# Full segments alone: half 0's memory sums in four matmuls, the sums' banks exchanged, token sums by halves, a quarter of the second values on VectorE

## The chip, the cores and the metric

The kernel runs on one core of one Trainium2 chip. The metric is the device time of one execution in microseconds (us). TensorE is called PE in the profile's lines (PEld are its weight loads), VectorE is DVE, ScalarE ACT, GpSimd POOL and SyncE SP.

## The reference

Two layers, each an attention with a recurrent memory and then a gated mixer over the sequence; inputs are bf16, the sequence has 2048 tokens of width 512.

```python
def _A_ref(x, mem0, Wq, Wk, Wv, Wo, seg_len):        # 32 heads of 128, 8 memory rows, seg_len 32
    mem = mem0
    for s in range(n_seg):                            # 64 segments, one after the other
        h = jnp.concatenate([mem, x[:, s*seg_len:(s+1)*seg_len]], axis=1)      # 40 rows
        q, k, v = (jnp.einsum('btd,dhe->bhte', h, W) for W in (Wq, Wk, Wv))
        scores = jnp.einsum('bhqe,bhke->bhqk', q, k) * Dh ** (-0.5)
        p = _softmax(jnp.where(mask[None, None], scores, -1e9), axis=-1)
        o = jnp.einsum('bhte,hed->btd', jnp.einsum('bhqk,bhke->bhqe', p, v), Wo)
        mem = o[:, :M, :]                             # the memory of the next segment
        outs.append(o[:, M:, :])
...
x = x + _A_ref(_layernorm(x), ...)
x = x + _B_ref(_layernorm(x), ...)                    # gated mixer over the sequence
x = x + _A_ref(_layernorm(x), ...)
x = x + _B_ref(_layernorm(x), ...)
```

The mask lets each row see the 8 memory rows and the tokens up to itself. The softmax needs, for every head and query row, the sum of the exponentials over the keys; that sum is what the change touches.

## The kernel before, in words

The attention pass `a_block` runs twice (`first` is true for the first pass). It goes through 64 segments (`s`), four to a block of 128 rows (`tb = s // 4`, `j4 = s % 4`, 16 blocks). A segment needs the memory rows that the segment before it left, so segments run one after the other. TensorE, VectorE and ScalarE run their instructions in the order in which the program issues them. The order within a segment is written out by hand in `segment`, with work of the next block or of the output product put between its steps: three calls of `fill()` take such work from a generator. In full segments (below) they yield 4, 8 and 20 matmuls of 512 columns.

The 32 heads are handled as two halves `r` of 16 heads. In a segment, in order:

- queries and keys of both halves (`qk`, into `psQ`, `psm`, `psK`), copied by ScalarE and turned by VectorE;
- scores of half 0 into `psS`, ScalarE's exponential into `S` (`exps`, L1123), VectorE's mask product into `E` (`close`, L1126); values of half 0 from `psK` to `VA[:, 0]` by VectorE (L1212);
- values of half 1 into `psV` in four steps over the contraction, with the scores of half 1 and then `sums_zero` (L1137) between them. `sums_zero` sums half 0's exponentials for the 8 memory query rows: sixteen matmuls on 128x32 tiles with the constant `half`, into the free end of the `psS` bank;
- ScalarE: logarithm of those sums (`inverse`, L1180), copy of half 1's values to `VA[:, 1]` (L1227), exponential of minus the logarithm (L1181), which gives their inverse in `Rm`; VectorE: `close(1)`;
- the first `fill()`; `pv(0)`, the product of weights and values of half 0 (L1163, and L1166 for the memory rows' keys), into `psO[0]`; `sums_tokens` (L1155), the sums of both halves for the token rows into `psT`, four matmuls on 64x128 tiles with the constant `ones`; `sums_one` (L1146), the memory sums of half 1, four such matmuls, into the columns 320 to 384 of `psO[1]`; `pv(1)` into `psO[1]`;
- VectorE's `memory_out(0)` (L1184), the memory rows of half 0 times `Rm`, into `uT`; `spare1`, work of other blocks on VectorE and GpSimd; the second `fill()`; ScalarE's `inverse` of half 1; `memory_out(1)`;
- the output product of the memory rows: `wo_pairs` (L946, half 0's heads, into `px`) and `wo_rest` (L953, half 1's heads, into columns 384 to 512 of `psO[1]`); then the fold of its parts, the next segment's memory rows, and the token rows (`tok_out`, `last_out`).

Each of `psO[0]` and `psO[1]` is a pair of PSUM banks. The framework puts a wait between instructions of different engines that touch the same PSUM memory; where the kernel knows better it says so by hand. Line 1055 does that for two copies out of `px` that read different partitions, one by ScalarE and one by VectorE:

```python
m = nc.vector.tensor_copy(cross[64:128, :], px[0:64, 128:256])
tc.declare_no_dep(m.ins, beside.ins, reason="other partitions of the tile")
```

In the first pass some blocks take parts of their product from an earlier stage:

```python
light = first and tb + 1 < NB and (tb + 1) // 4 in EARLY        # EARLY = (2, 3)
```

Of the kernel before, what the change touches and what calls it, by code (L numbers as in the profile page):

```python
# [717 lines left out]
def a_block(tc, c, rows, front, MV_in, RS_in, MV_out, RS_out, ahead, wo, S, first):  # L718
    nc = tc.nc
# [5 lines left out]
    with ExitStack() as ctx:  # L725
# [39 lines left out]
        def other_bank(mms, *reads):  # L765

            for m in mms:
                for r in reads:
                    tc.declare_no_dep(m.ins, r.ins, reason="another bank of the tile")
# [301 lines left out]
        def segment(s, fill, spare1, spare2, spare3, tail, loads):  # L1071
# [21 lines left out]
            def v_mm(r, ps, kts=range(KT)):  # L1093
                return mm_chunk(ps, lambda kt, cg: hA_cur[:, kt, :], lambda kt, cg: cols_rhs(w, 4 + r, kt, cg), kts)
# [30 lines left out]
            def close(r):  # L1125
                nc.vector.tensor_tensor(out=E[:, r], in0=S[:, r].unsqueeze(1).to_broadcast([P, 2, 224]), in1=maskN[:], op=ALU.mult)  # L1126

            def e_all(e, lo, hi):

                return e[:, :, 0:160].rearrange("p n (i q) -> p n i q", q=40)[:, :, :, lo:hi]  # L1130

            def e_own(e, b):
                return e[:, :, 160:224].rearrange("p n (i b e) -> p n i b e", i=4, b=2)[:, :, :, b, :]

            def sums_zero(pN):

                return [nc.tensor.matmul(pN[32 * cg:32 * cg + 32, 64 * g:64 * g + 64], lhsT=half[:, g, :], rhs=e_own(E[:, 0], 0) if k else e_all(E[:, 0], 0, 8),  # L1137
                                         start=False, stop=True, tile_position=(0, 32 * cg), skip_group_check=True)
                        for k in range(2) for g in range(2) for cg in range(4)]

            def sums_one():

                for k in range(2):
                    for g in range(2):
                        e = E[64 * g:64 * g + 64, 1]
                        nc.tensor.matmul(psO[1][:, g, 320:384], lhsT=ones[64 * g:64 * g + 64, :], rhs=e_own(e, 0) if k else e_all(e, 0, 8),  # L1146
                                         start=(k == 0), stop=True, skip_group_check=True)

            def sums_tokens(ps):

                for k in range(2):
                    for g in range(2):
                        e = E[64 * g:64 * g + 64].rearrange("p r s n -> p (r s) n")
                        o = ps[:, g, :].rearrange("p (n i q) -> p n i q", n=4, i=4)
                        nc.tensor.matmul(o[:, :, :, 24:32] if k else o, lhsT=ones[64 * g:64 * g + 64, :],  # L1155
                                         rhs=e_own(e, 1) if k else e_all(e, 8, 40), start=(k == 0), stop=True, skip_group_check=True)

            def pv(r):

                for i in range(4):  # L1160
                    for g in range(2):
                        o = psO[r][:, g, 0:320].rearrange("p (s i q) -> p s i q", s=2, i=4)[:, :, i, :]
                        nc.tensor.matmul(o, lhsT=VA[64 * g:64 * g + 64, r, i, :], rhs=E[64 * g:64 * g + 64, r, :, 40 * i:40 * i + 40],  # L1163
                                         start=(r == 0 and i == 0), stop=True, skip_group_check=True)
                for g in range(2):
                    nc.tensor.matmul(ends(heads40(psO[r][:, g, 0:320])), lhsT=VX[64 * g:64 * g + 64, j4, r, :],  # L1166
                                     rhs=E[64 * g:64 * g + 64, r, :, 160:224], start=False, stop=True, skip_group_check=True)
# [10 lines left out]
            def inverse(r, src):  # L1178
                rm = Rm[:, r]
                nc.scalar.activation(out=rm, in_=src, func=ACT.Ln)  # L1180
                return lambda: nc.scalar.activation(out=rm, in_=rm, func=ACT.Exp, scale=-1.0)  # L1181
# [26 lines left out]
            expd = exps(0)  # L1208
# [10 lines left out]
            other_bank(scores(1), expd)  # L1219
            expd = exps(1)  # L1220
            v_mm(1, psW, (2,))
            pN = psS[:, 0, 224:352]
            other_bank(sums_zero(pN), expd)
            v_mm(1, psW, (3,))
            Rm = segp.tile([P, 2, 2, 64], F32, name="Rm", bufs=1)
            invert = inverse(0, pN.rearrange("p (g q) -> p g q", g=2))
            nc.scalar.copy(VA[:, 1].rearrange("p i e -> p (i e)"), psW[:])  # L1227
# [101 lines left out]
        for s in range(NSEG):  # L1329
# [164 lines left out]
```

## Time and profile before

| | |
|---|---|
| median of 3 runs | 1601.4 us (1600.6 to 1609.43) |
| the profiled execution's own time | 1603.44 us |
| its span, first to last instruction | 1601.7 us |
| mean granted TensorE clock | 0.998 |

In the page, the first block gives each engine's busy time and its share of the span. The chain of waits is followed back from the last instruction: at each step to what released it, or to the instruction before it on its engine. In lists in order of time each line has the start and the length in us, the engine, the kernel's line, the operation, the tiles (out<-in), shapes and the count of instructions put together; a bracket gives idle time of the engine before it and what ended it. TensorE's matmuls are pipelined, so their lengths overlap.

### The profile page before, as it was taken

To read this page: it belongs to the slowest core of one execution; us is meant where nothing else is said; L and a number is where in the kernel's file an instruction comes from. 1 tells how busy PE (TensorE), PEld (TensorE's weight loads), DVE (VectorE), ACT (ScalarE), POOL (GpSimd) and SP (SyncE) were. 2 spreads that over 40 slices of the span, in tenths; PEclk is the share of its full clock that TensorE was granted. 3 is DMA by queue.
4 is the path that set the end of the run, shared out by engine and by line. 5 is a ranking of instruction groups with operands and counts; after the bars stand their busy time and mean duration, and the time that the engine had idled before them with its cause. 6 is when DMAs were issued, how large, how long until landed. Compare 5 with 4: busy or idle time off the path is not lost.

```text
span 1601.7 us, 90904 instructions
## 1 busy us (share of the span) xinstructions
PE 1578.5 (99%) x41046; PEld 977.2 (61%) x41046; DVE 1086.1 (68%) x3094; ACT 1050.9 (66%) x2279; POOL 306.8 (19%) x674
## 2 busy tenths in 40 slices
PE   7999999999999999999999999999999999999999
PEld 3566666666666666666656666666666666665565
DVE  4666777777777777784456666666777677767722
ACT  4677777777777777670057777777777777776400
POOL 6211121112211222320021111111222122224000
PEclk9999999999999999999999999999999999999999
DMA  9322111122211332378951111111222123416697
GB/s 361 132 58 42 44 40 37 44 41 80 74 53 41 87 87 61 102 177 170 207 170 45 45 48 48 41 40 41 67 86 67 40 66 87 89 50 179 146 193 163
DMA packets 240540, 145.99 MB, mean 91 GB/s; under 512 B 173272, under 2 KB 215872, under 8 KB 240152
## 3 DMA queue, kind: packets, MB, share of 16 engines
q1 hardware_dynamic: 226232, 94.00, 25.9%
q0 software_dynamic: 13920, 46.18, 8.6%
q8 instruction: 321, 5.26, 1.3%
q14 instruction: 67, 0.55, 0.1%
HBM read 60.21 MB, written 39.55 MB: 62 GB/s over the span
## 4 chain that ended last, share of the span: by engine, by line
PE 94%; DMA 2%; DVE 2%; issue 1%; ACT 1%; POOL 0%; DVEq 0%; SPq 0%; POOLq 0%; ACTq 0%
PE psQ L762 14%; PE psK L762 13%; PE psb L762 10%; PE pg L403 9%; PE psO L953 7%; PE px L946 7%; PE psm L762 7%; PE psV L762 7%; PE pwB L965 3%; PE psO L1163 3%; PE pz L302 3%; PE psT L1155 2%; PE py L446 2%; PE psS L1114 2%; PE psS L1137 1%; PE psO L1166 1%
## 5 line engine op out<-in xcount | busy, mean ns | idle before, releaser
L762 PEld LDWEIGHTS <-hT 128*32 128x32 bf16 x12288 | 339.4, 97 | 262.3 <-DVE hT L1063 18.3
L762 PE MATMUL psV<-Wv_sb,hT 128*32 128x512 bf16 x2048 | 165.8, 379 | 0.0
L1088 ACT CAST rows<-psQ 128x512 bf16<-128x512 f32 x256 | 144.3, 589 | 21.2 <-PE psQ L762 17.5
L1184 DVE TENSOR_TENSOR uT<-psO,Rm 128x128 bf16<-128x128 f32 x256 | 74.7, 292 | 122.7 <-ACT Rm L1181 121.6
L1123 ACT ACTIVATE S<-psS 128x224 bf16<-128x224 f32 x256 | 92.2, 360 | 97.4 <-PE psS L1118 97.4
L1091 DVE STREAM_TRANSPOSE KA<-rows 128x256 f32<-128x256 f32 x256 | 113.0, 441 | 61.9 <-ACT rows L1088 59.4
L403 PE MATMUL pg<-z,wspT 128*128 128x344 bf16 x1024 | 154.3, 310 | 0.0
L1187 DVE TENSOR_TENSOR uT<-psO,Rt 128x384 bf16<-128x384 f32 x256 | 140.3, 548 | 18.8 <-ACT Rt L1266 17.4
L762 PE MATMUL psK<-Wv_sb,hT 128*32 128x512 bf16 x2048 | 151.7, 378 | 0.0
L1266 ACT ACTIVATE Rt<-Rt 128x512 f32<-128x512 f32 x256 | 147.3, 622 | 4.0
L1091 DVE STREAM_TRANSPOSE QQ<-rows 128x256 f32<-128x256 f32 x256 | 112.5, 440 | 49.0 <-ACT rows L1088 46.1
L953 PE MATMUL psO<-Wo_high,uT 128*32 128x128 bf16 x8192 | 140.5, 220 | 2.1 <-issue 1.1
L762 PE MATMUL psQ<-Wq_sb,hT 128*32 128x512 bf16 x2048 | 135.0, 380 | 0.5 <-issue 0.5
L946 PE MATMUL px<-Wo,uT 128*32 128x256 bf16 x3840 | 134.7, 274 | 0.3
L762 PE MATMUL psQ<-Wk_sb,hT 128*32 128x512 bf16 x2048 | 134.6, 379 | 0.0
L762 PE MATMUL psK<-Wk_sb,hT 128*32 128x512 bf16 x2048 | 134.5, 379 | 0.0
L762 PE MATMUL psm<-Wq_sb,hT 128*32 128x512 bf16 x2048 | 134.5, 379 | 0.0
L403 PEld LDWEIGHTS <-wspT 128*128 128x128 bf16 x1024 | 100.0, 98 | 53.5 <-issue 0.4
L1263 ACT ACTIVATE Rt<-psT 128x1024 f32<-128x1024 f32 x127 | 130.0, 1024 | 3.1
L953 PEld LDWEIGHTS <-uT 128*32 128x32 bf16 x8192 | 123.2, 97 | 12.1 <-issue 3.2
L946 PEld LDWEIGHTS <-uT 128*32 128x32 bf16 x4096 | 105.2, 97 | 23.5 <-issue 1.2
L1045 POOL COPY KX<-old 128x128 bf16<-128x128 bf16 x128 | 64.7, 533 | 259.2 <-PE psS L1118 202.1
(224 smaller groups left out, 2909.3 us busy)
## 6 DMA issues: line engine op xcount, KB each, us to landing
o_d<-o_sb SPq DMA_DIRECT2D x126, 64.0 KB
vb_d<-front SPq DMA_DIRECT2D x31, 256.0 KB
VX<-vb_d SPq DMA_DIRECT2D x124, 64.0 KB
ln_x<-xd SPq DMA_DIRECT2D x26, 256.0 KB
y_o<-o_d POOLq DMA_DIRECT2D x22, 256.0 KB, 3.4
xd<-y_o POOLq DMA_DIRECT2D x22, 256.0 KB, 3.0
Wq_sb<-in_A_Wq_dram POOLq DMA_DIRECT2D x8, 512.0 KB, 7.5
Wk_sb<-in_A_Wk_dram POOLq DMA_DIRECT2D x8, 512.0 KB, 9.5
```

The lines of the kernel that those rows point to most:

```text
L403: nc.tensor.matmul(pg[t][:, k, 0:344], lhsT=wsp[t][:, st, :], rhs=z(st, 344 * k, 344 * k + 344), start=(st == 0), stop=(st == NT - 1))
L762: return [nc.tensor.matmul(ps[32 * cg:32 * cg + 32, :], lhsT=lhs(kt, cg), rhs=rhs(kt, cg), start=(kt == 0), stop=(kt == KT - 1), tile_posi ...
L946: nc.tensor.matmul(px[at:at + 32, 0:256], lhsT=lhs[:, h, :], rhs=wo_rhs(h, slice(k + 2, None, -2) if h % 2 else slice(k, None, 2)), start= ...
L953: nc.tensor.matmul(pw[32 * cg:32 * cg + 32, :], lhsT=lhs[:, h, :], rhs=wo_rhs(h, cg), start=False, stop=(h == H - 1), tile_position=(0, 32 ...
L1045: eng.tensor_copy(KX[r][:].rearrange("p g (k i) -> p i g k", i=4), bs["KTB"][:, r].rearrange("p (i g) k -> p i g k", i=4)[:, :, :, 8 * j4: ...
L1088: return r, mms, copy(r[:].rearrange("p (n el two) -> p n el two", n=8, two=2), ps.rearrange("p (n two el) -> p n el two", n=8, two=2))
L1091: nc.vector.transpose(out=(QQ[:, j % 2, :, 0:32] if j < 2 else KA[:, j % 2]).bitcast(F32).rearrange("p n q one -> p n (q one)"), in_=r[:]. ...
L1123: return nc.scalar.activation(out=S[:, r], in_=psS[:, r, 0:224], func=ACT.Exp, scale=scale)
L1184: nc.vector.tensor_tensor(out=hview(uT_cur[:], r, 24, 32), in0=oview(r, 0, 8), in1=Rm[:, r].rearrange("p g (n q) -> p g n q", q=8), op=ALU ...
L1187: nc.vector.tensor_tensor(out=hview(uT_nxt[:], r, 0, 24), in0=oview(r, 8, 32), in1=rview(r, 0, 24), op=ALU.mult)
L1263: nc.scalar.activation(out=Rt[:], in_=psT[:], func=ACT.Ln)
L1266: nc.scalar.activation(out=rt, in_=rt, func=ACT.Exp, scale=-1.0)
```

## The change

`segment` gets a flag `full`, true for `tb > 3 and not light`. Where it is false, the code is as before. Where it is true:

- `sums_zero` is left out. After the first `fill()`, ahead of `pv(0)`, `sums_memory(0)` computes the same sums by four matmuls with `ones` on 64x128 tiles.
- The sums change places: those of half 0 go to columns 320 to 384 of `psO[1]`, those of half 1 to the same columns of `psO[0]`.
- `sums_tokens` is issued for half 0, then come the memory sums of half 1, then `sums_tokens` for half 1: eight matmuls in place of four, each with half the columns.
- Three quarters of half 1's values (384 of 512 columns) are copied by ScalarE, the last quarter by VectorE after `close(1)`. The logarithm and the exponential of half 0's sums follow the copy on ScalarE.

```diff
-            def sums_one():
+            def sums_memory(r, ps, begun=False):
 
                 for k in range(2):
                     for g in range(2):
-                        e = E[64 * g:64 * g + 64, 1]
-                        nc.tensor.matmul(psO[1][:, g, 320:384], lhsT=ones[64 * g:64 * g + 64, :], rhs=e_own(e, 0) if k else e_all(e, 0, 8),
-                                         start=(k == 0), stop=True, skip_group_check=True)
-
-            def sums_tokens(ps):
+                        e = E[64 * g:64 * g + 64, r]
+                        nc.tensor.matmul(ps[:, g, :], lhsT=ones[64 * g:64 * g + 64, :], rhs=e_own(e, 0) if k else e_all(e, 0, 8),
+                                         start=(k == 0 and not begun), stop=True, skip_group_check=True)
+
+            def sums_tokens(ps, lo=0, hi=2):
 
                 for k in range(2):
                     for g in range(2):
-                        e = E[64 * g:64 * g + 64].rearrange("p r s n -> p (r s) n")
-                        o = ps[:, g, :].rearrange("p (n i q) -> p n i q", n=4, i=4)
+                        e = E[64 * g:64 * g + 64, lo:hi].rearrange("p r s n -> p (r s) n")
+                        o = ps[:, g, 256 * lo:256 * hi].rearrange("p (n i q) -> p n i q", n=2 * (hi - lo), i=4)
                         nc.tensor.matmul(o[:, :, :, 24:32] if k else o, lhsT=ones[64 * g:64 * g + 64, :],
-                                         rhs=e_own(e, 1) if k else e_all(e, 8, 40), start=(k == 0), stop=True, skip_group_check=True)
+                                         rhs=e_own(e, 1) if k else e_all(e, 8, 40), start=(lo == 0 and k == 0), stop=True, skip_group_check=True)
...
             v_mm(1, psW, (2,))
-            pN = psS[:, 0, 224:352]
-            other_bank(sums_zero(pN), expd)
-            v_mm(1, psW, (3,))
             Rm = segp.tile([P, 2, 2, 64], F32, name="Rm", bufs=1)
-            invert = inverse(0, pN.rearrange("p (g q) -> p g q", g=2))
-            nc.scalar.copy(VA[:, 1].rearrange("p i e -> p (i e)"), psW[:])
-            invert()
-            close(1)
+            if full:
+                v_mm(1, psW, (3,))
+                close(1)
+                nc.scalar.copy(VA[:, 1, 0:3].rearrange("p i e -> p (i e)"), psW[:, 0:384])
+                nc.vector.tensor_copy(VA[:, 1, 3], psW[:, 384:512])
+            else:
...
             if not begin:
                 fill()
+            sums = [psO[1 - r if full else r][:, :, 320:384] for r in range(2)]
+            if full:
+                sums_memory(0, sums[0])
+                inverse(0, sums[0])()
             pv(0)
             psT = att.tile([P, 2, 512], F32, name="psT")
-            sums_tokens(psT)
-            sums_one()
+            if full:
+                sums_tokens(psT, 0, 1)
+                sums_memory(1, sums[1], begun=True)
+                sums_tokens(psT, 1, 2)
+            else:
+                sums_tokens(psT)
+                sums_memory(1, sums[1])
             pv(1)
             memory_out(0)
             spare1(E)
             if not begin:
                 fill()
-            inverse(1, psO[1][:, :, 320:384])()
+            inverse(1, sums[1])()
             memory_out(1)
...
-            segment(s, lambda n=1: [next(more, None) for _ in range(n)], spare1, spare2, spare3, tail, loads)
+            segment(s, tb > 3 and not light, lambda n=1: [next(more, None) for _ in range(n)], spare1, spare2, spare3, tail, loads)
```

More of the change, by code (lines that the diff above doesn't have):

```diff
@@ L1069, in store_o, with segment @@
             nc.sync.dma_start(o_d[SEG * (s - 1):SEG * s, :].rearrange("r (cg c) -> cg r c", cg=4), o_sb[:])
-        def segment(s, fill, spare1, spare2, spare3, tail, loads):
+        def segment(s, full, fill, spare1, spare2, spare3, tail, loads):
             tb, j4 = s // 4, s % 4
@@ L1221, in segment @@
             v_mm(1, psW, (2,))
-            pN = psS[:, 0, 224:352]
-            other_bank(sums_zero(pN), expd)
-            v_mm(1, psW, (3,))
             Rm = segp.tile([P, 2, 2, 64], F32, name="Rm", bufs=1)
-            invert = inverse(0, pN.rearrange("p (g q) -> p g q", g=2))
-            nc.scalar.copy(VA[:, 1].rearrange("p i e -> p (i e)"), psW[:])
-            invert()
-            close(1)
+            if full:
[4 more added lines that the diff above has]
+            else:
+                pN = psS[:, 0, 224:352]
+                other_bank(sums_zero(pN), expd)
+                v_mm(1, psW, (3,))
+                invert = inverse(0, pN.rearrange("p (g q) -> p g q", g=2))
+                nc.scalar.copy(VA[:, 1].rearrange("p i e -> p (i e)"), psW[:])
+                invert()
+                close(1)
             psO = [attO[r].tile([P, 2, 512], F32, name="psO") for r in range(2)]
```

## The prediction

> **What bounds the kernel now.** First the page: who is busy, and which engine the chain of waits runs through.
>
> ```profile
> PE 1578.5 (99%) x41046; PEld 977.2 (61%) x41046; DVE 1086.1 (68%) x3094; ACT 1050.9 (66%) x2279; POOL 306.8 (19%) x674
> ...
> PE 94%; DMA 2%; DVE 2%; issue 1%; ACT 1%; POOL 0%; DVEq 0%; SPq 0%; POOLq 0%; ACTq 0%
> ```
>
> TensorE carries 94% of the chain and is busy nearly always, while VectorE and ScalarE have a third of their time free. That is an average over both attention passes and the mixers between them, so next comes the stretch that the change touches most: the full segments of the second pass, by windows.
>
> ```profile
> core 0 of [0], span 1601.7 us
> ...
> 976.40:1460.50 484.10, 483.34 (x14791) 303.31 (x14784) 353.48 (x1019) 361.21 (x806) 103.10 (x225) 1.00 0.24 64
> ```
>
> Of 484.10 us TensorE (the first pair) is busy in 483.34, at a granted clock of 1.00. So here a removed matmul is worth its place in TensorE's stream, and a wait of TensorE costs its whole length; work on ScalarE and VectorE is free until it makes TensorE wait. The question is narrow: how much stream goes away, and does anything new arrive late. For both I follow one undisturbed full segment (second pass, segment 41), first its pieces in the chain of waits. A piece runs from the end of what came before to its own end, so its length is what the group costs the stream.
>
> ```profile
> 1233.06 0.12 PE psS L1137 x16
> ...
> 1233.91 0.30 PE psT L1155 x4
> 1234.22 0.06 PE psO L1146 x4
> 1234.28 0.14 PE psO L1163 x8
> ```
>
> Then the same segment in order of time, one engine after the other (start us, length us; a group's length holds the drain of its last member, about 0.2 us, so steps are read from start to start).
>
> ```profile
> 1232.89 0.29 PE L1137 MATMUL psS<-E,half 128*32 128x64 bf16 x16
> 1233.00 0.39 PE L762 MATMUL psV<-Wv_sb,hT 128*32 128x512 bf16 x4
> 1233.22 0.39 PE L762 MATMUL psb<-Wq_sb,hB 128*32 128x512 bf16 x4
> ...
> 1233.54 0.32 PE L1163 MATMUL psO<-E,VA 64*128 64x80 bf16 x8
> ...
> 1234.05 0.22 PE L1146 MATMUL psO<-E,ones 64*128 64x64 bf16 x4
> 1234.11 0.31 PE L1163 MATMUL psO<-E,VA 64*128 64x80 bf16 x8
> ...
> 1234.40 0.62 PE L762 MATMUL psb<-Wq_sb,hB 128*32 128x512 bf16 x8
> 1234.85 1.04 PE L946 MATMUL px<-Wo,uT 128*32 128x256 bf16 x30
> ...
> 1235.72 1.07 PE L953 MATMUL psO<-Wo_high,uT 128*32 128x128 bf16 x64
> ```
>
> ```profile
> 1233.77 0.12 PEld L1155 LDWEIGHTS <-ones 64*128 64x128 bf16 x4
> ...
> 1235.61 1.00 PEld L953 LDWEIGHTS <-uT 128*32 128x32 bf16 x64
> ```
>
> ```profile
> 1232.93 0.36 ACT L1123 ACTIVATE S<-psS 128x224 bf16<-128x224 f32 x1 [0.75 <-PE psS L1118]
> 1233.24 0.28 ACT L1180 ACTIVATE Rm<-psS 128x128 f32<-128x128 f32 x1
> 1233.44 0.58 ACT L1227 CAST VA<-psV 128x512 bf16<-128x512 f32 x1
> 1233.93 0.31 ACT L1181 ACTIVATE Rm<-Rm 128x128 f32<-128x128 f32 x1
> 1234.52 0.28 ACT L1180 ACTIVATE Rm<-psO 128x128 f32<-128x128 f32 x1 [0.28 <-PE psO L1166]
> 1234.82 0.31 ACT L1181 ACTIVATE Rm<-Rm 128x128 f32<-128x128 f32 x1
> 1235.94 0.26 ACT L1050 COPY cross<-px 64x128 f32<-64x128 f32 x1 [0.81 <-PE px L946]
> ```
>
> ```profile
> 1232.60 0.68 DVE L1212 CAST VA<-psK 128x512 bf16<-128x512 f32 x1
> 1233.32 0.39 DVE L1126 TENSOR_TENSOR E<-S,maskN 128x448 bf16<-128x448 bf16 x1
> 1234.27 0.29 DVE L1184 TENSOR_TENSOR uT<-psO,Rm 128x128 bf16<-128x128 f32 x1 [0.56 <-ACT Rm L1181]
> 1235.17 0.29 DVE L1184 TENSOR_TENSOR uT<-psO,Rm 128x128 bf16<-128x128 f32 x1 [0.60 <-ACT Rm L1181]
> 1235.94 0.28 DVE L1054 COPY cross<-px 64x128 f32<-64x128 f32 x1 [0.49 <-PE px L946]
> ```
>
> What to see: two deadlines of TensorE are already tight. The token sums read both halves' weights, and their first load of `ones` (1233.77) comes 0.06 us after VectorE closed half 1 (1233.32 + 0.39 = 1233.71). And the load of half 1's `uT` for the last output heads (L953, 1235.61) comes 0.15 us after the second `memory_out` ended (1235.17 + 0.29 = 1235.46).
>
> **The change part by part.** The condition holds in 64 of the 128 segments: blocks 4 to 15 of the second pass (48), and blocks 4, 5, 6 and 15 of the first (16). Everything else keeps its code. All costs are per full segment.
>
> *TensorE's stream.* Sixteen matmuls of L1137 leave: minus 0.12. Four of the shape that L1146 has come in for half 0: plus 0.06. They stand right ahead of the first `pv`, which uses the same 64-row tiles, so no change of tile shape is added. The token sums become two sets of four: the same columns, so I take 0 more; the high end is four more starts at 0.06 / 4 = 0.015 each, 0.06, and the low end 0. The wait on half 1's weights goes: the token sums of half 0 need only half 0, and the first reader of half 1 then comes a good 0.1 us after 1233.77. Its worth: 512 columns stream in 0.22 (psV at 1233.00 to psb at 1233.22), so the 512 and 128 columns that psT needs, two matmuls abreast, take 0.22 x 640 / 512 = 0.275 of the piece's 0.30. I take 0.02 for the wait (ends 0.02 and 0.03). Sum: -0.12 + 0.06 - 0.02 = -0.08, ends -0.09 and -0.02. TensorE alone would gain 64 x 0.08 = 5.1 us, 0.3%.
>
> *The second values, split.* `VA` of half 1 now starts when psV is done: its last matmuls ended at 1233.39, now 0.12 earlier, 1233.27, but ScalarE's exponential ends at 1233.29, so about 1233.32. For 384 columns I interpolate between 128 (0.28, L1180) and 512 (0.58): 0.48 (ends 0.45 and 0.58). End 1233.80. The other 128 columns on VectorE: between the 0.28 of L1054 and the 0.68 for 512 columns of L1212, nearest the first: 0.28. When can it start? VectorE is free at about 1233.7. But the two copies read one PSUM bank in the same partitions. L1050 and L1054 do start together on one bank (both 1235.94), in different partitions, and only because line 1055 takes away, by hand, an order that would otherwise hold. The change takes none away. So I put VectorE's copy behind ScalarE's: 1233.80 + 0.03 (a hand-over, as 1232.93 + 0.36 to 1233.32) + 0.28 = 1234.11, seen by TensorE 0.06 later, 1234.17. The second `pv` needs it for its seventh matmul, which stood at 1234.11 + 6/8 of 0.14 = 1234.21. Released at 1234.17, it is still 0.04 earlier than before; of the 0.08, 0.04 is lost here.
>
> The Trainium skill, PSUM — Partial Sum Buffer, section "PSUM bank collisions raise a hardware error", states that two engines must not touch the same bank and quadrant at once, reads against reads included. By that rule the order I assume must be kept by someone; the rows here show only the permitted case, different partitions.
>
> *The sums' banks exchanged.* Half 0's sums go to half 1's bank pair, so `pv(1)` must wait until ScalarE's logarithm has read them. Sums start at 1233.54 - 0.12 = 1233.42, last result 0.22 later (L1146's length), read 0.06 later (1232.89 + 0.29 to 1233.24): logarithm 1233.70 to 1233.98, behind the shorter `VA` copy, which has left ScalarE's input by then. `pv(1)` may start at 1234.04; it would arrive at 1234.11 - 0.08 = 1234.03. Behind it on TensorE stand the second fill and the output matmuls; cost 0 to 0.02, swallowed by the wait for the seventh matmul. Then the exponential, 1234.01 to 1234.32, and `memory_out(0)`, 1234.35 to 1234.64, 0.08 later than before. Its reader px starts at 1234.85 - 0.04: the eight fill matmuls from 1234.40 cover it; without them it would cost 0.2.
>
> Half 1's sums now lie in half 0's banks, ready before `pv(1)`, so its logarithm no longer waits for `pv(1)` (L1166). But VectorE's `memory_out(0)` reads the same banks, earlier in program order. If that order is kept: logarithm 1234.67 to 1234.95, exponential 1234.98 to 1235.29, `memory_out(1)` 1235.32 to 1235.61, seen at 1235.67. That is 0.15 later than before and ends the slack of the second deadline. TensorE would be ready for L953 at 1235.72 - 0.04 = 1235.68. A load that no longer runs ahead costs some 0.01 to 0.03 more. So of the 0.04 left, 0.01 to 0.05 goes here. Behind the logarithm on ScalarE wait only its exponential and, at 1235.94, the fold's copy: free in time.
>
> *Sum:* -0.08 + 0.04 + 0.03 = -0.01 per segment, times 64 = -0.6 us. DMAs, SyncE's and GpSimd's queues keep their order. The profiled execution took 1603.44 us (span 1601.7 and 1.7 around it), so by its own rows it comes to 1602.8; the median of the three runs is 2.0 lower, at 1601.4, and the forecast for it is 1600.8.
>
> **The rivals.**
>
> A. *No order between the readers of a bank.* VectorE copies its quarter right after closing half 1, and half 1's logarithm starts right after half 0's exponential. Then only half 0's logarithm holds `pv(1)`, by 0 to 0.02: -0.08 + 0.02 = -0.06, times 64 = -3.8 us: 1597.6. For it: nothing in the rows shows such a wait, since in this part of the segment no two engines read the same partitions of a bank before the change. Against it: line 1055. The Trainium skill's rule above speaks against it too: such reads would collide.
>
> B. *Slower: the second `memory_out` decides.* Same order as my forecast, but the serial chain through the exchanged bank (logarithm, exponential, product, logarithm, exponential, product) ends later than 1235.67. From there each hundredth is paid 64 times. Should the `VA` copy of 384 columns keep its 0.58, half 0's logarithm moves back to about 1233.79 and the end to 1235.76: 0.09 past the point, about +0.08 per segment, +5.1 us: 1606.5. For it: six dependent steps with hand-overs that I know to 0.01 or 0.02 each. Against it: the ScalarE rows scale with columns (0.28, 0.36 and 0.58 for 128, 224 and 512).
>
> C. *The sums do not get cheaper.* Four matmuls of 64 columns cost as much as the sixteen, which run four abreast. Then only the waits are left, all of them paid: +0.06 - 0.01 = +0.05, times 64 = +3.2 us: 1604.6. Against it: the piece of L1146 is half that of L1137.
>
> **How the numbers follow.** My forecast 0.58, A 0.22, B 0.16, C 0.04. A measurement of this kernel can tell about 0.5%, 8 us, from no change, which is 0.125 us per full segment. No case gains that: even the whole -0.09 makes 5.8 us. Faster by over 0.5% therefore gets 0.03, for scatter between runs (one run before stood at 1609.43). Slower by over 0.5% needs B with 0.13 instead of 0.08; 0.08, a part of B and scatter. The rest, 0.89, is no change that can be told. The range goes from A's likely end with the whole TensorE gain, 1596.5, to B's 1606.0. The forecast's own range, 0.03 per segment either way for the hand-overs and the token sums, is 1599 to 1603.
>
> **What would show it.** L1137's count should halve (sixteen in each segment that keeps it, 64 segments), `psO<-E,ones` go from 512 to 768 matmuls and `psT<-E,ones` likewise. In a full segment the chain piece of half 0's sums should read 0.06, and no load of `ones` should follow VectorE's E by 0.06. ScalarE's `VA<-psV` with 384 columns should take 0.48. Mine against A: VectorE's `VA<-psV` starts 0.03 after ScalarE's ends (A: right after E), and the second `Rm<-psO` is released by VectorE's `uT` (A: it follows the first exponential). If L953's first load follows `memory_out(1)` by about 0.06, the second deadline is the bound, and what lies past 1235.67 is B. A difference outside these places, or a full segment that changes by more than 0.1 us, would make the reasoning wrong.

## The result: 0.2% slower, and the profile after

The changed kernel took 1607.28 us in the median (1604.2 to 1613.03), the kernel before on the same chip 1603.88 (1600.59 to 1609.43): ratio 1.0022, 95% interval 1.0012 to 1.0033, about 3.5 us slower. Run again, it came to 1.0026 (1.0014 to 1.0039). The profiled execution took 1610.6 us, its span 1607.9, at a granted clock of 0.998.

The page of the changed kernel, engines and chain of waits:

```profile
PE 1577.9 (98%) x40534; PEld 974.7 (61%) x40534; DVE 1104.4 (69%) x3158; ACT 1053.4 (66%) x2279; POOL 307.6 (19%) x674
...
PE 90%; DMA 6%; DVE 2%; issue 1%; ACT 1%; POOL 0%; POOLq 0%; DVEq 0%; SPq 0%
```

TensorE is busy 0.6 us less, as a saving would have it, yet the span is 6.1 us longer. DMA has 6% of the chain where it had 2%, but that row misleads: 44 us of it are weight loads in the first 51 us, where the chain merely took another way through the same start (in the chain the queries of the first pass's second segment begin at 52.15 us after and at 53.10 before). So the first question is whether the segments grew or something else. One undisturbed full segment in windows, first of the changed kernel, then of the kernel before (us, then busy time and count of PE, PEld, DVE, ACT, POOL, the clock, DMA share, GB/s):

```profile
1240.75:1250.77 10.02, 10.02 (x304) 6.43 (x300) 7.32 (x22) 7.58 (x18) 0.48 (x1) 1.00 0.10 23
```

```profile
1237.69:1247.72 10.03, 10.03 (x312) 6.24 (x308) 7.01 (x21) 7.69 (x18) 0.48 (x1) 1.00 0.11 25
```

The median over 40 full segments of the second pass is 10.014 us after and 10.031 before, and 10.011 and 10.036 in a second pair of profiles: the change saves 0.02 us per full segment, 1.3 us in 64. The chain of waits in that segment shows of which pieces this is made, after and then before:

```profile
1246.60 0.17 PE psO L1146 x4
1246.76 0.14 PE psO L1163 x8
...
1246.96 0.14 PE psT L1155 x4
1247.10 0.06 PE psO L1146 x4
1247.16 0.14 PE psT L1155 x4
1247.30 0.20 PE psO L1163 x8
...
1248.10 0.87 PE px L946 x32
1248.98 0.89 PE psO L953 x64
```

```profile
1243.09 0.12 PE psS L1137 x16
...
1243.64 0.25 PE psO L1163 x8
...
1243.95 0.30 PE psT L1155 x4
1244.25 0.06 PE psO L1146 x4
1244.30 0.14 PE psO L1163 x8
...
1245.05 0.87 PE px L946 x32
1245.92 0.89 PE psO L953 x64
```

Half 0's sums and `pv(0)` together went from 0.12 + 0.25 to 0.17 + 0.14, minus 0.06. (The first group on 64-row tiles after 32-column tiles takes 0.11 more than a later one, 0.25 against 0.14 and 0.17 against 0.06; before that was `pv(0)`, now it is the sums. So the sums' own piece reads 0.17 and not the 0.06 that the prediction named as its sign.) The token sums went from 0.30 to 2 x 0.14, minus 0.02. `pv(1)` went from 0.14 to 0.20, plus 0.06. `px` and the last output heads keep 0.87 and 0.89. Sum: -0.02. Why `pv(1)` grew, and whether the second deadline holds, is in the order of time of the same segment:

```profile
1246.43 0.48 ACT L1226 CAST VA<-psV 128x384 bf16<-128x384 f32 x1
...
1246.94 0.29 DVE L1227 CAST VA<-psV 128x128 bf16<-128x128 f32 x1
...
1247.79 0.28 ACT L1180 ACTIVATE Rm<-psO 128x128 f32<-128x128 f32 x1 [0.36 <-DVE uT L1184]
...
1248.44 0.29 DVE L1184 TENSOR_TENSOR uT<-psO,Rm 128x128 bf16<-128x128 f32 x1 [0.69 <-ACT Rm L1181]
...
1248.78 0.69 PEld L953 LDWEIGHTS <-uT 128*32 128x32 bf16 x48
```

VectorE's quarter starts 0.03 us after ScalarE's copy has left the bank (1246.43 + 0.48 = 1246.91), and half 1's logarithm waits for VectorE's `uT`. Both readers' orders are kept, as forecast. The load of half 1's heads follows `memory_out(1)` by 0.05.

So the loss lies outside the segments. Cut at the start of the last segment, the part from there to the end of the span (the tail below) takes 156.1 us after and 151.3 before: 4.8 of the 6.1 us. (Of the rest 0.4 arises ahead of the second pass and 1.0 in its segments, where stalls of these two executions outweigh the saving.) TensorE's waits in that stretch of the changed kernel hold one that the kernel before did not have in this profile:

```profile
PE pz L302 <- DMA front<-xb_d: 2.6, 1, 2.6
```

That is the hand-over from the second attention to the second mixer: `pz` needs rows that go through a chain of stores and loads by SyncE and GpSimd. Here is that chain, GpSimd's instructions in order of time. Before (the last segment starts at 1450.48):

```profile
1463.75 0.56 POOL L234 DMA_DIRECT2D xd<-y_o  x1 [0.30 <-POOL y_o L233]
1464.31 0.54 POOL L227 DMA_DIRECT2D y_x<-xd  x1
1464.84 1.06 POOL L227 DMA_DIRECT2D wspL<-xd  x2
1469.13 0.62 POOL L229 DMA_DIRECT2D wspL<-o_d  x1 [3.23 <-DMA xb_d<-ln_xn]
```

After (the last segment starts at 1451.80):

```profile
1464.35 0.56 POOL L234 DMA_DIRECT2D xd<-y_o  x1 [0.30 <-POOL y_o L233]
1464.91 0.54 POOL L227 DMA_DIRECT2D y_x<-xd  x1
1465.44 1.06 POOL L227 DMA_DIRECT2D wspL<-xd  x2
1473.09 0.54 POOL L229 DMA_DIRECT2D wspL<-o_d  x1 [6.59 <-DMA o_d<-yB]
```

SyncE issues the two last stores of `yB`, which that load of `wspL` from `o_d` has to wait for, before:

```profile
1462.88 1.36 SPq L959 DMA_DIRECT2D o_d<-yB  x2
```

and after:

```profile
1464.31 1.36 SPq L959 DMA_DIRECT2D o_d<-yB  x2
```

Counted from the segment's start, SyncE's pair comes at 12.40 and 12.51 us, nearly alike. GpSimd's store of `xd`, with three loads of 256 KB behind it, comes at 13.27 before and at 12.55 after. Before, it followed the second store of `yB` (13.13); after, it runs ahead of it (13.24), and the load that needs `yB` starts at 21.29 in place of 18.65. The bracket of the load before names another store, SyncE's next; the packets in the trace show that `yB` counts there too. Its rows are 96 packets of 2048 bytes on SyncE's queue. The last of them ended at 17.61 before and at 20.25 after, and the load started 1.04 us later both times. What follows (row sums, their norms, the transposes for `pz`) is late by about that much.

The wait of 2.6 is not all of the 4.8. Right behind it the granted clock was 0.50 for 3.4 us, and TensorE issued 8 matmuls where the second profile of the changed kernel (`after_again` below), which had the same wait and no such drop, issued 16. First the changed kernel, then after_again:

```profile
1497.40:1500.80 3.40, 3.04 (x8) 1.12 (x9) 2.96 (x17) 0.00 (x0) 0.00 (x0) 0.50 1.08 226
```

```profile
1495.00:1498.40 3.40, 3.06 (x16) 1.57 (x17) 2.96 (x17) 0.53 (x1) 0.00 (x0) 1.00 1.01 227
```

With TensorE busy for 3.04 us of that at half the clock, I estimate that it lost some 1.5 us, so wait and clock make about 4.1 of the 4.8.

### The profile page after: what moved, and what is told of

It is laid out like the page before. It is cut to its first block, busy times and chain, and to the rows that moved or that the text cites. A ratio compares the mean times of both kernels' runs of the same rounds, so it can differ in the third digit from the quotient of the medians.

```text
span 1607.9 us, 89861 instructions
## 1 busy us (share of the span) xinstructions
PE 1577.9 (98%) x40534; PEld 974.7 (61%) x40534; DVE 1104.4 (69%) x3158; ACT 1053.4 (66%) x2279; POOL 307.6 (19%) x674
## 4 chain that ended last, share of the span: by engine, by line
PE 90%; DMA 6%; DVE 2%; issue 1%; ACT 1%; POOL 0%; POOLq 0%; DVEq 0%; SPq 0%
PE psQ L762 14%; PE psK L762 14%; PE psb L762 10%; PE pg L403 9%; PE psO L953 7%; PE px L946 7%; PE psV L762 7%; PE psm L762 7%; PE pwB L965 3%; PE psO L1163 3%; PE psT L1155 2%; PE py L446 2%; PE psS L1114 2%; PE pz L302 1%; DMA Wk_sb<-in_A_Wk_dram 1%; PE psO L1146 1%
## 5 line engine op out<-in xcount | busy, mean ns | idle before, releaser
L762 PEld LDWEIGHTS <-hT 128*32 128x32 bf16 x12288 | 335.8, 96 | 259.7 <-DVE hT L1063 17.8
L762 PE MATMUL psV<-Wv_sb,hT 128*32 128x512 bf16 x2048 | 158.4, 379 | 0.0
L1187 DVE TENSOR_TENSOR uT<-psO,Rt 128x384 bf16<-128x384 f32 x256 | 140.1, 547 | 18.7 <-ACT Rt L1281 16.9
L762 PE MATMUL psK<-Wv_sb,hT 128*32 128x512 bf16 x2048 | 152.1, 378 | 0.0
L953 PE MATMUL psO<-Wo_high,uT 128*32 128x128 bf16 x8192 | 140.7, 219 | 3.5 <-issue 2.7
L953 PEld LDWEIGHTS <-uT 128*32 128x32 bf16 x8192 | 117.2, 97 | 19.3 <-issue 5.2
L946 PEld LDWEIGHTS <-uT 128*32 128x32 bf16 x4096 | 104.0, 96 | 23.3 <-DVE uT L1184 12.8
```

The source lines that it names most:

```text
L762: return [nc.tensor.matmul(ps[32 * cg:32 * cg + 32, :], lhsT=lhs(kt, cg), rhs=rhs(kt, cg), start=(kt == 0), stop=(kt == KT - 1), tile_posi ...
L946: nc.tensor.matmul(px[at:at + 32, 0:256], lhsT=lhs[:, h, :], rhs=wo_rhs(h, slice(k + 2, None, -2) if h % 2 else slice(k, None, 2)), start= ...
L953: nc.tensor.matmul(pw[32 * cg:32 * cg + 32, :], lhsT=lhs[:, h, :], rhs=wo_rhs(h, cg), start=False, stop=(h == H - 1), tile_position=(0, 32 ...
L1187: nc.vector.tensor_tensor(out=hview(uT_nxt[:], r, 0, 24), in0=oview(r, 8, 32), in1=rview(r, 0, 24), op=ALU.mult)
```

## The experiments

Theory T at first was: GpSimd's instructions come in another order, and that makes the tail. It had a ground: GpSimd is not among the engines whose order the kernel fixes, and in the last segment but one its order did change. Before it was the two weight loads (L178, L179) and then the store of `xd` from `VX`; after it is the store first. The rivals: P, scattered stalls of TensorE where its own instructions arrive late, and the prediction's B. Each run below stands beside runs of the kernel before on the same chip. `NB - 1` is the last block, `NSEG - 1` the last segment.

**The same two kernels again** (no edit).

> The changed kernel once more, for a second profile. Theory T (the loss sits in the hand-over from the second attention to the second mixer, because GpSimd's instructions around its block of loads come in another order) expects the same place again: from the start of the last segment to the end about 4.8 us more than before, and TensorE's third group of front transposes (pz<-front) held about 2.6 us by a DMA. Theory P (the loss is scattered stalls of TensorE, 0.2 to 1.2 us each, set by where instructions lie in the stream) expects the stalls above 0.3 us in the same segments as in the first profile (20, 25, 103, 105 of each the first pass and 246.6, 297.8, 416.5, 604.1 us by time). If they are scatter of single executions they move. Both: 3.5 us over before, ratio 1.002.

> The kernel before once more, as a control: ratio 1.000. By T its tail, from the start of the last segment, repeats to within 1 us; by P its stalls above 0.3 us lie where they lay (533.7, 572.7, 1339 us), by scatter elsewhere.

Ratios 1.0026 (1.0014 to 1.0039) and 1.0002 (0.999 to 1.0014). The tail was 154.7 after, with `pz` held 2.7 us, and 152.9 before. T's place repeats; B is out, since the segments are shorter. P's stalls repeat in part (below).

**The last block with the old code; the last block alone with the new.**

```diff
-            segment(s, tb > 3 and not light, ...)
+            segment(s, 3 < tb < NB - 1 and not light, ...)      # last_old
+            segment(s, tb == NB - 1, ...)                       # last_only
```

> The change everywhere but in the last block of each pass, 56 full segments in place of 64. GpSimd has its order of before around the last segments. T: the tail is as before and the 20 ns saved per full segment are left, 56 x 0.02 = 1.1 us faster than before, ratio 0.9993. P: nearly all moved instructions stay moved, so some 3 us slower, ratio 1.002. The prediction's rival B (the second product chain is late): 56/64 of the loss, ratio 1.002, with full segments longer than before.

> The change in the last block of each pass only, 8 full segments, with GpSimd's order as in the changed kernel. T: the tail's 4.8 us less 8 x 0.02, 4.6 us slower than before, ratio 1.003. P: hardly any instruction is moved, ratio 1.000. Rival B: 8/64 of the loss, 0.4 us, ratio 1.0003.

1.0005 (0.9991 to 1.002) and 1.0015 (1.0003 to 1.0026); tails 151.2 and 155.8. The long tail goes with the last block. The totals are less clear: last_only is slower by half of what T named (1.003), and the interval of last_old holds both T's ratio (0.9993) and nearly P's (1.002).

**GpSimd's order restored in the changed kernel, and swapped in the kernel before.**

```diff
 def spare1(E):
+    if s == NSEG - 2:                       # order_back: the claim and load_w(2), moved up from the end of spare1
+        nc.vector.memset(front.w_in_sb[:, 2, FH - 1:FH + 1], 0.0)
+        front.load_w(2)
...
 def spare2():                               # swap_before: the same lines, moved down to here
```

> The changed kernel with one VectorE instruction, the claim on the mixer's weight tile in the last segment but one, issued a little earlier, so that GpSimd's two weight loads (L178, L179) come ahead of its store of xd again, as in the kernel before; nothing else differs. Theory T (GpSimd's order around these loads makes the tail): the tail from the start of the last segment falls from about 155.5 to 151 to 153 us, and 64 x 0.02 us of saving remain: 1 us faster than before, ratio 0.9993. Theory P (scattered late instruction fetches): tail as the fetches fall, total still 3.5 us over before. A third, T2 (what counts is when the last segments run, not the order): tail stays at 155.5, ratio 1.0025.

> The kernel before with the same claim issued later, so that GpSimd's store of xd comes ahead of the two weight loads (and the load of y_x too). T: the tail grows from about 152 to 155 us, ratio 1.002. T2 and P: nothing moves, ratio 1.000.

1.0019 (1.0007 to 1.0031) with a tail of 155.4, and 0.9995 (0.9983 to 1.0008) with 151.4. (The claim is the small VectorE write on the mixer's weight tile that stands ahead of GpSimd's loads of it.) The order followed the edit in both and the tail did not. T falls: the order is without effect.

**The last 24 rows taken out of the late queues.**

```diff
-        for y in (NB - 6, NB - 5):
-            y_norm(y, nc.sync)
+        y_norm(NB - 6, nc.sync)
...
-                nc.gpsimd.dma_start(o_d[S - SEG:S - 8, :], o[0:24, :])
+                nc.sync.dma_start(o_d[S - SEG:S - 8, :], o[0:24, :])
...
+        y_norm(NB - 5, nc.sync)
```

> The changed kernel, GpSimd's order left as it is, but the last 24 output rows of the attention no longer stand in the queues that are late: VectorE adds them ahead of the last normalisation, and SyncE stores them instead of GpSimd. T: the collision of GpSimd's transfers with the stores of yB remains, but the last load of the row sums no longer waits for it twice; TensorE's third group of front transposes is not held, tail 151.2, and with 64 x 0.02 saved the kernel is some 2 us faster than before, ratio 0.9988. P: tail as it was apart from chance, ratio 1.002.

> The kernel before with the same two moves of the last 24 rows. T: its tail, 151.2 and 152.9 in two profiles, goes to 151.2: some 0.5 to 1 us faster, ratio 0.9996; and the changed kernel with the moves is 1.3 us faster than this one, which is the change by itself. P: ratio 1.000.

1.0063 (1.0041 to 1.0085) and 1.0062 (1.0038 to 1.0086): misses by 12 and 11 us. Tails 161.1 and 160.1. GpSimd's rows of fix_after:

```profile
1475.22 0.54 POOL L229 DMA_DIRECT2D xo<-o_d  x1
1476.21 0.54 POOL L229 DMA_DIRECT2D y_o<-o_d  x1
1476.74 0.54 POOL L229 DMA_DIRECT2D wspL<-o_d  x1
```

The edit let the loads of `xo`, `y_o` and `wspL` start together, with `y_o` second. VectorE, which adds `y_o` first and in order, got it about 9 us after its issue. It looks as if starting more transfers at once delayed the one that is needed first; no run tests that by itself. The same edits also lengthened the hand-over after the first attention, by 3 us.

**GpSimd's load of y_o released later** (it was issued 0.9 us later). The order being out, the new theory T3 is a race: whether GpSimd's store of `xd` (released by its add, and that by the landing of `y_o`) is issued ahead of the last store of `yB`.

```diff
-                if s == NSEG - 1:                                  # in spare1
-                    y_load(NB - 5, rows.pool.tile([P, DM], F32, name="y_o")[:])
-                    rows.y_add(NB - 5, first, nc.gpsimd, nc.gpsimd)
...
+                if s == NSEG - 1:                                  # at the end of spare2
+                    o = rows.pool.tile([P, DM], F32, name="y_o")[:]
+                    nc.vector.memset(o[:, 0:1], 0.0)
+                    y_load(NB - 5, o)
+                    rows.y_add(NB - 5, first, nc.gpsimd, nc.gpsimd)
```

> The changed kernel with one edit in the last segment: GpSimd's load of y_o (the row sum of the fifth block from the end) is released some 0.7 us later, by a one-column VectorE write behind memory_out(1); the order of every queue stays. Theory T3 (GpSimd's order is without effect; the tail is a race: if GpSimd's store of xd and its next three loads are issued ahead of the last stores of yB, these land at 20.5 to 21 us from the start of the segment in place of 16 to 18.5, and all that follows is late): the store of xd is now issued after the stores of yB, the first load of wspL from o_d starts at 16 to 19 us in place of 21, the tail falls from 155.5 to 151.3, and the kernel is 1.3 us faster than before, ratio 0.999. Rival T2 (something else of the changed last segments is slow): the tail stays at 155 and the ratio at 1.002.

> The kernel before with the same edit. T3: the tail, 151.2 to 152.9 us in three profiles, becomes 151.3 each time: ratio 0.9995 to 1. T2: ratio 1.000. The pair's difference, late_y_after against this, is the change without the tail: T3 1.3 us faster, ratio 0.999.

0.9997 (0.9982 to 1.0012) and 1.0003 (0.9991 to 1.0016): in this run the changed kernel is level with the kernel before once this one load is later (its repeat is below). Its rows (the last segment starts at 1451.00):

```profile
1464.30 0.60 POOL L234 DMA_DIRECT2D xd<-y_o  x1 [0.30 <-POOL y_o L233]
...
1470.02 0.60 POOL L229 DMA_DIRECT2D wspL<-o_d  x1 [3.52 <-DMA xb_d<-ln_xn]
```

The store is at 13.30, now behind `yB` (13.23), the load from `o_d` starts at 19.0 in place of 21.3, and the tail is 153.0. The last packet of `yB` ended at 17.98 in place of 20.25. T3 stands for the tail, which is still 1.7 us longer than it named (`pz` held 1.1); the gain of 1.3 us over the kernel before that it also named did not show.

**The copy of the second values whole; the token sums by halves alone.**

```diff
-                nc.scalar.copy(VA[:, 1, 0:3].rearrange("p i e -> p (i e)"), psW[:, 0:384])
-                nc.vector.tensor_copy(VA[:, 1, 3], psW[:, 384:512])
+                nc.scalar.copy(VA[:, 1].rearrange("p i e -> p (i e)"), psW[:])     # whole_copy
```

> The changed kernel with all 512 columns of half 1's values copied by ScalarE, as before. The seventh product of pv(1) no longer waits for VectorE, but half 0's logarithm starts about 0.12 us later behind the longer copy, and with it everything up to memory_out(1). The prediction's reading of the second deadline (each hundredth past it is paid in every segment) expects full segments of 10.11 to 10.13 us in place of 10.01, 64 x 0.11 = 7 us slower than the changed kernel, ratio to before about 1.006. If the second deadline has slack after all: 9.98 to 10.01, ratio 1.002 or less.

In halves_only the old code of the full segments stays but for the lines of `sums_tokens` and of half 1's sums between them.

> The kernel before with one part of the change alone, in its full segments: token sums half by half (eight matmuls for four), half 1's memory sums between them; sums of half 0 in sixteen matmuls, banks and the copy of the values as before. The prediction's term: 0.02 us of waiting for half 1's weights goes, four more matmuls cost 0 to 0.06: full segments 10.01 to 10.07 us in place of 10.03, the lower end the likelier. Total between 1.3 us faster and 2.6 slower, ratio 0.999 to 1.002, with a tail as before.

1.004 (1.0027 to 1.0054) and 1.0002 (0.9993 to 1.0011). The first is below the 1.006 that was expected, the second within its range. One full segment each, whole_copy and then halves_only:

```profile
1040.11:1050.22 10.11, 10.11 (x305) 6.09 (x301) 7.01 (x21) 7.82 (x18) 0.48 (x1) 1.00 0.09 24
```

```profile
1039.04:1049.05 10.01, 10.01 (x316) 6.25 (x312) 7.01 (x21) 7.69 (x18) 0.48 (x1) 1.00 0.10 24
```

The segments are as expected, but the 0.10 that the whole copy costs is not mostly the second deadline. The pieces of that segment which grew:

```profile
1046.63 0.27 PE psO L1163 x8
...
1048.38 0.93 PE psO L953 x64
```

`pv(1)` takes 0.27 where the changed kernel has 0.20: it now waits from its first product on, until half 0's logarithm, itself behind the longer copy, has read the exchanged bank. That is 0.07; the second deadline (0.93 for 0.89) has 0.04. So both are met to within a few hundredths in the changed kernel and no more. The halves alone give four fifths of what the whole change gives: the lower quartile of the second pass's full segments is 10.030 before, 10.014 with the halves and 10.010 with the change.

**Which of the last segments; and the change without the race.** only_127 has the change in the last segment of the second pass alone, only_124 in the three before it; last_halves is last_old with the token sums by halves in the last block too; late3 is late_y_after with its lines placed behind the sum of the fold; late_y_again is late_y_after once more.

> The change in the last segment of the second pass alone. GpSimd's order is that of the kernel before. If the last segment itself makes the difference (its stores of yB come later by 0.1 us, its load of y_o too), the first load of wspL from o_d starts at about 21 us and the tail is about 155. If the three segments before it make it, as 16 to 19 us and 151.5.

> The change in the three segments before the last alone. If they make the difference (GpSimd's load of y_x for the last row sum but one starts 0.6 us later and takes 3.1 us in place of 3.8 to 4.8, so that its chain arrives earlier), the tail is about 155; if the last segment does, about 151.5.

> The change in all full segments but those of the last block of each pass, which have only the token sums by halves. T3: the last block's transfers keep their distance from the stores of yB, tail 151.3 to 151.6; of the steady saving 56 x 0.02 + 8 x 0.015 = 1.2 us remain: ratio 0.999 to before, faster than both kernels. If the tail alone is not the loss: ratio 1.001 or more, as the one run of the change without the last block (1.0005) would allow.

> The changed kernel with GpSimd's load of y_o in the last segment released still later, behind the sum of the fold (L1056) on VectorE, 1.3 us after its place in the changed kernel; queue orders unchanged. T3: the store of xd comes 0.5 us or more after the last store of yB, the first load of wspL from o_d starts at about 16.3 us, TensorE's front transposes are not held, tail 151.3; with 64 x 0.02 saved, 1.5 us faster than before, ratio 0.999, and the fastest of all. If the saving is lost elsewhere: 1.000 or more.

> late_y_after once more. T3: ratio 0.9995, tail 151.3 to 153 us; if the first result was chance and the loss is not the tail: 1.002.

The tails of only_127 and only_124, one execution each, were 151.2 and 151.4: neither part made the long tail by itself. Of the two answers that each expectation named, each run gave the one that points at the other part; which step of the four segments shifts GpSimd stays open. last_halves came to 1.0017 (1.0004 to 1.0031), a miss: a segment with a 1.9 us stall just ahead of the last put the store back in front of `yB` in its profile (12.54 against 13.22; tail 153.0), but that is one execution. late3: 1.0006 (0.9994 to 1.0019), tail 151.7 with `pz` not held; the race is gone, the saving does not show. late_y_again: 1.0013 (1.0001 to 1.0025), tail 152.5, slower than the first time and than expected. Taken together, the two late_y kernels' runs lie 0.7 ± 1.1 us above the kernel before in the mean and the two sets of the changed kernel 3.2 ± 1.1 (95%): 2.5 less, where their tails are 2.7 shorter. So the total agrees with the tail.

All profiles but the two with the 24 rows moved, from the start of the last segment, ordered by the first column; a negative first number says that GpSimd's store of `xd` was issued ahead of SyncE's second store of `yB` (all in us):

| kernel | store of xd minus last yB | last packet of yB | first wspL from o_d | pz held | tail |
|---|---|---|---|---|---|
| late3 | +1.07 | 15.41 | 16.33 | no | 151.7 |
| halves_only | +0.74 | 15.53 | 16.41 | no | 151.5 |
| last_old | +0.61 | 15.38 | 16.27 | no | 151.2 |
| only_124 | +0.27 | 15.56 | 16.45 | no | 151.4 |
| late_y_again | +0.19 | 17.68 | 18.71 | 0.95 | 152.5 |
| before | +0.14 | 17.61 | 18.65 | no | 151.3 |
| late_y_after | +0.07 | 17.98 | 19.01 | 1.10 | 153.0 |
| only_127, late_y_before | -0.11 | 17.81, 17.91 | 18.85, 18.96 | no | 151.2, 151.4 |
| swap_before | -0.38 | 17.59 | 18.47 | no | 151.4 |
| after_again | -0.58 | 20.00 | 21.04 | 2.66 | 154.7 |
| last_halves | -0.68 | 19.95 | 20.99 | 1.17 | 153.0 |
| after, whole_copy | -0.69 | 20.25, 20.20 | 21.29, 21.23 | 2.62, 1.72 | 156.1, 153.9 |
| before_again | -0.71 | 19.53 | 20.57 | 1.26 | 152.9 |
| order_back | -0.84 | 20.12 | 21.15 | 2.13 | 155.4 |
| last_only | -0.94 | 19.84 | 20.77 | 2.58 | 155.8 |

The first three columns go together without exception: half a microsecond or more ahead of `yB`, and the load starts at 20.6 to 21.3; a quarter or more behind it, and it starts at 16.3 to 16.5; always 0.9 to 1.1 us after the last packet of `yB`. Even the kernel before lost the race once, and its tail was 1.6 us longer. The last columns follow less strictly. The three longest tails of the table (after, last_only, order_back) are those in which the granted clock fell to 0.5 for 3.4 us around the end of the wait; after_again waited as long without that.

## Why the prediction was wrong, point by point

- **The stream of TensorE** was right: -0.06 for half 0's sums (-0.12 + 0.06) and -0.02 for the token sums, and four more starts cost nothing.
- **The second values, split**: mechanism right, size off. 384 columns took 0.48, VectorE followed 0.03 behind, the seventh product waited; it cost 0.06, not 0.04. That also settles rival A: the order between readers of a bank is there. The Trainium skill, PSUM — Partial Sum Buffer, section "PSUM bank collisions raise a hardware error", forbids such reads at once. The trace shows the order kept, with 0.03 us from one reader's end to the other's start in each full segment; no run here shows what reads at once would do.
- **The sums' banks exchanged**: the order was right, the price too high. `memory_out(1)` ends 0.18 later in the segment than before (0.15 forecast), but the output heads' piece stayed at 0.89, so nothing was paid where 0.03 was forecast. The 0.01 to 0.03 for a load that no longer runs ahead stood on no row; here the load starts 0.02 ahead of the first matmul (1248.78 and 1248.80) and cost nothing that shows. In whole_copy, 0.1 later, 0.04 was paid there, and 0.07 at the wait for the logarithm, which the forecast put at 0 to 0.02 and which is free only as long as the copy is short.
- The segment came to -0.02 where -0.01 was forecast, -1.3 us in all. Rivals B and C have no share in it. That it came close is in part luck: 0.02 too little for the second values and 0.03 too much for the second deadline nearly cancel.
- **The step that failed** is the one sentence after the sum: "DMAs, SyncE's and GpSimd's queues keep their order", and with it that 64 times a segment is the whole. The order of GpSimd did change; order_back shows that this was harmless. What the forecast put at nothing without a reason is time: the queues' transfers in the last block were not set against each other. GpSimd's store is released by the landing of `y_o` and SyncE's stores by VectorE, and in the kernel before they were 0.14 us apart. That row could have been read. The prediction's last line had said that a difference outside the segments would make it wrong; it did. Shown in its place: the tail is some 3.5 us longer with the change in all of the last block, because `yB` lands some 2.5 us later, and one load issued 0.9 us later takes most of that back. Why GpSimd arrives earlier is known only in part (next point).
- **What stays open.** From the issue of GpSimd's load of `y_o` to its add it took 2.8 to 3.4 us with the change in the whole last block (four profiles), 3.1 to 4.6 with the old code there (five). It landed the sooner the earlier GpSimd's load of `y_x` ahead of it was issued: 2.6 to 3.3 us after its own issue where `y_x` was issued 2.7 to 5.4 us from the segment's start (nine profiles), 3.3 to 4.4 where that was 5.5 to 6.3 (six; the late_y kernels and late3 left out, since there the load of `y_o` itself is moved). No run moves `y_x` alone, and what moves it is not known. By tail and segments alone the changed kernel should be some 2.0 us slower (tails 155.4 against 152.1, means of two profiles each, less 1.3); the means of all runs differ by 3.3 ± 1.7 and 3.1 ± 1.5 (95%), which does not exclude 2.0. The five kernels that have the change nearly everywhere without the longest tail lie at 0.9997 to 1.0017, in the mean 1.0008, where T3 expected 0.999 to 0.9995. A microsecond or two in them was not found; the stalls below scatter by more than that from one execution to the next. No version came out clear of noise faster than the kernel before.
- The base counts too: the three runs given had a median of 1601.4, later runs of the kernel before 1602.3 to 1604.8. Of the 6.5 us between the forecast of 1600.8 and the 1607.28 measured, 2.5 are the base, 0.6 the gain that did not show and 3.4 the slowdown. The forecast's 0.5% as what a measurement can tell was too coarse: these intervals are 0.1 to 0.2% wide to either side.
- Two ends of the range are off from their own sums: B was worked out to 1606.5 and enters as 1606.0, and A with the whole TensorE gain of 5.1 us gives 1596.3, not 1596.5. Neither changes the account.

## What to carry to other kernels

A saving of 0.02 us in a loop is smaller than what a shift of the last iterations can set off behind the loop, so the hand-over belongs to the sum: look there for two queues whose transfers are issued within a microsecond of each other, and ask which of them the next stage waits for. Compare two profiles first by pieces of the program and not by engines; here the loop showed a gain and the stretch behind it the loss. And before a queue order is blamed, restore it alone.

## What the runs showed of the hardware

What is issued just ahead of a transfer can cost more time than the transfer itself. The stores of `yB` are 192 KB and are issued in 1.36 us in both kernels. From the issue of the second store to its last packet it took 2.3 us in late3, where GpSimd's 1 MB begins 1.07 us behind it, 4.5 in the kernel before (0.14 behind) and 7.0 in the changed kernel (0.69 ahead); the load that waits for them starts at 16.3, 18.7 and 21.3. The Trainium skill, DMA: Bandwidth & Descriptors, section "Issuing engines are not separate DMA queues", says that DMAs from SyncE, ScalarE and GpSimd run on the same 16 engines and interleave; these rows agree.

The granted clock fell to 0.5 for 3.4 or 6.8 us around the end of six of the seven waits of 2.1 us or more that TensorE has in the tails of all profiles (after, last_only, order_back, fix_after twice, fix_before), and of none of the shorter ones there. The seventh, 2.66 us in after_again, had no drop, so the length of the wait alone does not decide it.

TensorE's own instructions come by DMA, as the counts below show, and now and then late. The page of the changed kernel has a queue whose packets fit them, and a stall looks like this (the bracket gives the idle time):

```profile
q8 instruction: 317, 5.19, 1.3%
```

```profile
246.15 0.67 PE L953 MATMUL psO<-Wo_high,uT 128*32 128x128 bf16 x33
247.32 0.63 PE L953 MATMUL psO<-Wo_high,uT 128*32 128x128 bf16 x31 [0.50 <-issue]
```

Its 81,068 matmuls and weight loads over 317 packets are 256 a packet; before, 82,092 over 321 are 256 too. In five profiles (both of each kernel and last_old) all 30 matmuls of L953 on which TensorE stalls with the bracket "issue" lie a multiple of 256 of TensorE's instructions apart (within one, its semaphore instructions counted), they start 1.2 to 1.6 us after the end of such a packet, and some are the same instruction from profile to profile (segment 45: 0.24, 0.26 and 0.26 us in the two profiles of the changed kernel and in last_old). Summed over an execution, what the segments take above their own tenth percentile over all profiles is 9 to 17 us, with old code and with new. This is the scatter in which a saving of 1.3 us cannot be seen in the totals, and the reason to read it from undisturbed segments.
